# Scores of all chunks on VectorE, first loads and first Gram matrices spread over queues and banks, and a new order, in a fused deltanet and mixture-of-depths kernel

## The chip, the cores and the metric

The kernel runs on one core of a Trainium2 chip, in fp32. The metric is device time in microseconds, the median of the runs. The engines are PE (TensorE, matrix multiply), DVE (VectorE), ACT (ScalarE), POOL (GpSimd) and SP (SyncE, which issues DMAs).

## What is computed

Two blocks in a row. The first is a delta rule over 768 steps for 4 batches and 8 heads of width 48; its output, with the heads side by side, is x of width 384. The second takes, in each batch, the 128 tokens with the highest score, and runs these alone through a feed-forward network.

```python
k_n = k / (np.linalg.norm(k, axis=-1, keepdims=True) + 1e-06)
for t in range(S):
    kt, vt, bt = (k_n[:, :, t], v[:, :, t], beta[:, :, t, None])
    y[:, :, t] = np.einsum('bhd,bhde->bhe', q[:, :, t], state)
    v_old = np.einsum('bhde,bhd->bhe', state, kt)
    state = state + bt[:, :, :, None] * np.einsum('bhd,bhe->bhde', kt, vt - v_old)
x = np.ascontiguousarray(y.transpose(0, 2, 1, 3)).reshape(B, S, H * D)
scores = np.einsum('bsd,d->bs', x, w_gate)
for b in range(B):
    top_idx = np.argpartition(-scores[b], capacity)[:capacity]
    xe = x[b, top_idx]
    ye = np.maximum(xe @ w1, 0.0) @ w2
    g = 1.0 / (1.0 + np.exp(-scores[b, top_idx]))
    out[b, top_idx] = x[b, top_idx] + g[:, None] * ye
```

## The kernel before

**Tiling.** The sequence is cut into chunks of 64 steps. Two batches make a group, so there are 2 groups of 12 chunks: 24 chunks i, of 16 independent states (8 heads x 2 batches) each. Inside a chunk the 64 steps are solved at once, by inverting a triangular 64x64 matrix for each state. The inversions are done for four chunks together: six epochs e, of chunks 4e to 4e+3.

**Preparation of a chunk.** `load` (L655) brings k, q and v; PE transposes k (L666), ACT copies the result out as kt (L671). `products` (L716) multiplies the keys with each other, the Gram matrices, and with the queries. For epochs 1 to 5 the Gram matrices are copied to gs, spilled to DRAM and read back transposed as tile a. For epoch 0 this is done on the chip: `mm_g0` (L694) writes them to two PSUM banks, `out_g0` copies them to tile tt, one bank by DVE (L703, L708) and one by ACT (L703, L705, L706), and `turn_in` (L779) transposes them into a. The banks come from a ring "boot" of two entries, the banks prec and py, and the two halves of ap. A chunk gives its entry back when both engines have copied.

**An epoch.** The diagonal of a is read (L790 in epoch 0 on DVE, L825 on POOL afterwards), its root taken (ACT, L794), scales, strengths and a reciprocal formed (L830 to L839), a is scaled (L843), a table laid out (L808) and multiplied with it (L848, L849). This chain is POOL's, but for the root and the reciprocal. ACT lifts the result into PSUM (L856), and DVE eliminates: 30 pairs of a product (L878) and a subtraction (L885), each on the result of the one before. Then the solution is turned out (L866) and back (L898). POOL copies parts of it (lows, L1006, eight pieces, two for each chunk) for the join of the blocks of each chunk on PE (z, j) and ACT (L994, L1000).

**Recurrence of a chunk.** POOL scales v (L1032), PE multiplies with the state (L1040), DVE adds (L1047), PE applies the inverse (L1053), ACT copies (L1058), PE updates the state (L1064), and PE and ACT make x (L1080, L1091, L1097), which SP writes out (L1102). Then each token's score is the sum of x times w_gate: for chunks 0 to 21 POOL multiplies (L1114) and ACT sums (L1118), for the last two DVE does both in one instruction (L1110).

**Ranking and network, per group.** Each score is compared with all others of its batch by masks mk (POOL, L1199 with L1203; some by DVE), counted by ACT (L1217) and PE (sums, L1227), added up (L1233); the rank (L1265, L1266) is compared with a row of 1 to 128 (choose, L1269), which gives the indices (L1288, L1292, L1294). POOL gathers the chosen rows (L1309), DVE scores them again for the gate (rescore, L1297), PE runs both layers (mm_1 L1325, mm_2 L1339), DVE adds (L1344), POOL scatters (L1349).

**The order.** Nothing is scheduled by the compiler. Each operation is entered in a `Plan` with an engine, a cost, its dependencies and a due time, which two tables, SHIFT by kind of operation and PART by kind and place, move. A list scheduler lays the operations out on each engine with these numbers, and fills idle PE at the start with matmuls on a constant (filler, L577). The instruction streams are then written in that order, and each engine works through its own in order. DMA issues stand on SP's stream, some on ACT's or POOL's.

## Time and profile before

| | us |
| --- | --- |
| runs | 314.04, 312.94, 309.76 |
| median | 312.94 |
| the profiled execution | 311.51 |
| its span in the profile | 309.8 |
| PE, ACT, DVE, POOL busy in it | 266.2, 198.3, 187.3, 179.8 |
| mean granted clock of PE | 0.94 |

The span is what the profile shows, from the first to the last record; the time of an execution has some 1.7 us around it. A timeline row gives a start, a duration, engine, line, operation, what it writes and reads, and in brackets how long the engine was idle just before, with what released it. A group row gives the total, the mean of one in ns, and the idle time before the group's instructions. Line numbers are those of the kernel before.

### The profile page before, as it was taken

The numbers are of one execution on the slowest core, as the hardware profiler recorded it, in microseconds if no ns is written. First come the engines' busy times: TensorE is split into PE (matmuls) and PEld (weight loads), VectorE is DVE, ScalarE is ACT, GpSimd is POOL, SyncE is SP. The second block draws the span as 40 slices with busy tenths as digits, with TensorE's granted clock in tenths as the row PEclk, the third lists the DMA queues.
The fourth block names the chain that finished last, engine by engine and source line by source line (L and its number), as shares of the span: only waits on it lengthen the run. The fifth ranks groups of instructions, "written<-read, shape, count | busy, mean of one in ns | idle before, by whom it ended". The sixth has DMA issues, their size and how long they took to land.

```text
span 309.8 us, 14498 instructions
## 1 busy us (share of the span) xinstructions
PE 266.2 (86%) x6225; PEld 216.2 (70%) x6236; DVE 187.3 (60%) x518; ACT 198.3 (64%) x571; POOL 179.8 (58%) x258
## 2 busy tenths in 40 slices
...
GB/s 116 135 92 174 149 224 142 162 236 194 94 141 94 157 149 135 129 170 129 149 120 117 39 139 151 95 53 149 61 15 44 4 53 28 54 25 54 0 28 26
DMA packets 105889, 32.70 MB, mean 106 GB/s; under 512 B 98272, under 2 KB 102496, under 8 KB 105824
## 3 DMA queue, kind: packets, MB, share of 16 engines
...
q0 software_dynamic: 512, 1.57, 1.6%
q8 instruction: 49, 0.80, 1.1%
...
## 4 chain that ended last, share of the span: by engine, by line
PE 52%; ACT 15%; DVE 14%; issue 10%; POOL 4%; SPq 3%; DMA 2%; POOLq 0%; DVEq 0%; ACTq 0%
PE inv L716 6%; PE inv L666 6%; PE prec L1053 5%; DVE ap L885 5%; PE psta L1064 5%; DVE tmp L878 4%; PE ap L1339 4%; PE py L1080 4%; PE ap L1325 3%; PE py L1091 3%; ACT wbd L1058 3%; PE prec L1040 3%; PE inv L577 2%; SPq L655 2%; ACT tt L1000 2%
## 5 line engine op out<-in xcount | busy, mean ns | idle before, releaser
L885 DVE TENSOR_TENSOR ap<-ap,tmp 128x30 f32<-128x30 f32 (+9 forms) x180 | 60.8, 338 | 10.0 <-ACT a L861 3.8
L878 DVE TENSOR_TENSOR tmp<-a,ap 128x30 f32<-128x30 f32 (+9 forms) x180 | 58.8, 326 | 8.5 <-ACT ap L856 2.3
L738 POOL TENSOR_TENSOR p<-p,up 128x512 f32<-128x512 f32 x24 | 30.4, 1270 | 17.0 <-ACT p L732 16.9
L1199 POOL TENSOR_SCALAR mk<-rep 128x64 bf16<-128x64 f32 (+11 forms) x22 | 27.7, 1257 | 14.6 <-PE inv L1227 6.2
L1047 DVE TENSOR_TENSOR v<-v,prec 128x384 f32<-128x384 f32 x22 | 12.1, 549 | 32.6 <-ACT tt L1000 14.3
L1053 PE MATMUL prec<-v,tt 64*64 64x48 f32 x768 | 27.8, 220 | 4.2 <-POOL v L1032 1.5
L1053 PEld LDWEIGHTS prec<-v,tt 64*64 64x64 f32 x768 | 24.8, 134 | 8.5 <-DVE v L1047 3.7
L1058 ACT COPY wbd<-prec 64x384 f32<-64x384 f32 x48 | 22.7, 472 | 10.6 <-PE prec L1053 10.0
L1000 ACT COPY tt<-inv 32x128 f32<-32x128 f32 x96 | 24.4, 255 | 6.1 <-PE inv L993 4.5
L1006 POOL COPY tt<-tt 32x256 f32<-32x256 f32 x48 | 20.2, 422 | 11.9 <-DVE tt L866 8.4
L1032 POOL TENSOR_TENSOR v<-v,nnT 128x384 f32<-128x384 f32 x24 | 19.7, 831 | 11.6 <-DVE ap L885 9.7
L1064 PE MATMUL psta<-wbd,k 128*48 128x96 f32 x352 | 21.2, 264 | 4.9 <-ACT wbd L1058 4.7
L1114 POOL TENSOR_TENSOR prod<-x,wg 128x384 f32<-128x384 f32 x22 | 22.3, 1016 | 4.2 <-ACT x L1097 2.9
L1071 ACT COPY s<-psta 64x384 f32<-64x384 f32 x44 | 20.8, 472 | 4.2 <-PE psta L1064 3.6
L577 PE MATMUL inv<-warm 128*128 128x512 bf16 x57 | 20.3, 462 | 2.8 <-DVE warm L591 2.1
L1064 PEld LDWEIGHTS psta<-wbd,k 128*48 128x48 f32 x352 | 16.1, 130 | 8.5 <-ACT wbd L1058 7.6
L1349 POOL DMA_INDIRECT out_dram<-oe,idx x4 | 4.1, 1018 | 30.5 <-DVE oe L1344 24.9
L716 PE MATMUL inv<-qt,kt 48*64 48x64 f32 x768 | 19.1, 232 | 2.8 <-ACT qt L671 1.7
L1091 PE MATMUL py<-wbd,p 128*64 128x96 f32 x384 | 21.5, 255 | 0.0
L666 PE MATMUL inv<-ident,k 128*128 128x128 f32 x96 | 17.7, 315 | 3.5 <-issue 2.4
L1080 PE MATMUL py<-s,qt 128*64 128x96 f32 x352 | 19.7, 254 | 1.1 <-issue 1.0
L716 PEld LDWEIGHTS inv<-qt,kt 48*64 48x64 f32 x768 | 15.3, 141 | 6.4 <-ACT qt L671 3.0
(160 smaller groups left out, 633.0 us busy)
## 6 DMA issues: line engine op xcount, KB each, us to landing
...
q<-in_q_dram SPq DMA_DIRECT2D x48, 96.0 KB, 3.6
v<-in_v_dram SPq DMA_DIRECT2D x48, 96.0 KB, 3.3
k<-in_k_dram SPq DMA_DIRECT2D x44, 96.0 KB, 3.6
...
```

Source lines behind the costliest of these rows:

```text
L666: nc.tensor.transpose(ps[:, r * P:(r + 1) * P], x[:, 2 * r:2 * r + 2].rearrange("p b d -> p (b d)"), ident)
L716: nc.tensor.matmul(bank(keys[rt])[half[par], r], lhsT=kt[ds[rt], r, half[par]], rhs=x[ds[rt], r, half[par]], start=True, stop=True)
L738: nc.gpsimd.tensor_tensor(out=t, in0=t, op=ALU.mult, in1=up[:, None, :].to_broadcast([P, GP, C]))
L878: nc.vector.tensor_tensor(out=view(), op=ALU.mult, in0=got("a", e)[:, j + 1:, j:j + 1].to_broadcast([P, w, j]), in1=blocks[:, j:j + 1, :j] ...
L885: nc.vector.tensor_tensor(out=a[:, j + 1:, :j], in0=a[:, j + 1:, :j], in1=view(), op=ALU.subtract)
L1000: nc.scalar.copy(to[lo[par], :, int(w == "jb"), HC:], view(w)[lo[par]])
L1053: nc.tensor.matmul(pw[half[par], a], lhsT=tt[half[par], ch * GP + a], rhs=x[half[par], a], start=True, stop=True)
L1058: nc.scalar.copy(wb[half[par], :, par], pw[half[par]])
L1064: nc.tensor.matmul(psta[ds[a % 2], a // 2], lhsT=t[:, a, :D], rhs=wb[:, a].rearrange("p h d -> p (h d)"), start=(c == 0 and a < 2), stop=True,
L1080: nc.tensor.matmul(pyv[half[bb], h4, :, par], lhsT=qt[:, bb * 2 + h4, half[par]], rhs=s_old[:, bb * 2 + h4, par], start=(h4 == 0 and par = ...
L1091: nc.tensor.matmul(pyv[half[bb], h4, rt], lhsT=t[:, a], rhs=wb[:, a], start=(c == 0 and h4 == 0 and rt == 0), stop=True, skip_group_check= ...
L1199: nc.gpsimd.tensor_scalar(out=mk[:, :(j + 1) * C].rearrange("p (j c) -> p j c", c=C), in0=rep[:, :j + 1, :C], scalar1=rep[:, j, C:], scala ...
```

## The change

Line numbers from L790 on are 8 higher in the changed kernel, those of L738 and L716 5 higher. It does five things.

- The loads of k for chunks 0 and 1 go wholly to SP's queue, those of chunks 2 and 3 to ACT's; before, each of the four was split in halves between the two.
- The first Gram matrices of even chunks use the banks prec and py, those of odd chunks the first half of ap for DVE's copy and a bank of the ring inv for ACT's.
- The copies of the off-diagonal blocks by ACT become an operation of their own, `out_side` (L714), due 12 us later; the join's z of epoch 0 depends on it.
- All 24 scores are the single instruction on DVE (L1118).
- The planner has other costs, landing times and starts for each engine, other due times for the first operations, and new tables SHIFT and PART.

```diff
-LAND = 2.6
+LAND, EARLY, LATER = 2.4, 1.6, 6.0
+BEGIN = {"SP": 0.8, "ACT": 2.1, "DVE": 6.9, "POOL": 7.5, "PE": 2.1}
...
 SHIFT = {
-    "ACT:counts": -8.3, "ACT:ej": -53, "ACT:ez": -35.5, "ACT:gate0": 7.5, "ACT:lift": -50.6,
+    "ACT:counts": -2.9, "ACT:ej": -14.2, "ACT:ez": -3.1, "ACT:gate0": 8.6, "ACT:lift": -6.3,
...
-            self.lands.append(self.moved + LAND)
+            self.lands.append(self.moved + (LAND if t > LATER else EARLY))
...
-            free.setdefault(op.eng, 0.0)
+            free.setdefault(op.eng, BEGIN.get(op.eng, 0.0))
...
-    rings["boot"] = [[prec, py], [ap[:, m] for m in range(2)]]
-    plan.ring("boot", 2)
+    plan.ring("b0", 1)
+    rings["ap0"] = [ap[:, 0]]
+    plan.ring("ap0", 1)
...
+        def boot(rt):
+            x = [prec, py][rt] if i % 2 == 0 else got("inv", i, "boot") if rt else got("ap0", i)
+            return x[:, :GI * C].rearrange("p (r t) -> p r t", t=C)
+
...
                     if rt:
-                        put(to[hi[par], :, HC:], ps[hi[par], :, HC:])
-                        put(to[lo[par], :, :HC], ps[lo[par], :, HC:])
+                        put(to_g[hi[par], :, rt, HC:], ps[hi[par], :, HC:])
...
+        def out_side():
+            for par in range(2):
+                nc.scalar.copy(to_g[lo[par], :, 1, :HC], boot(1)[lo[par], :, HC:])
...
-        n["lk"] = sp(0.7 if first else 1.36,
-                     load(i, "k", (nc.sync, nc.scalar) if first else (nc.sync,) * 2),
-                     prio=u - 30, take=[("k", i)], dmas=2, room=None if first else 1.0)
-        if first:
-            act(0.7, lambda: None, [], u - 30)
+        if i in (2, 3):
+            n["lk"] = act(1.36, load(i, "k", (nc.scalar,) * 2), prio=u - 90, take=[("k", i)],
+                          dmas=2)
+        else:
+            n["lk"] = sp(1.36, load(i, "k", (nc.sync,) * 2), prio=u - (60 if first else 30),
+                         take=[("k", i)], dmas=2, room=None if first else 1.0)
...
-            n["g"] = pe(0.75, mm_g0, [n["ek"]], u, take=[kb], hard=True, ins=16 * GI)
-            n["eg"] = [dve(1.15, out_g0(0), [n["g"]], u, give=[kb], hard=True),
-                       act(1.0, out_g0(1), [n["g"]], u, give=[kb], hard=True)]
+            kb = [[("b0", i)], [("ap0", i), ("inv", i, "boot")]][i % 2]
+            n["g"] = pe(0.62, mm_g0, [n["ek"]], u - 100, take=kb, hard=True, ins=16 * GI)
+            n["eg"] = [dve(1.4, out_g0(0), [n["g"]], u - 100, give=kb[:1], hard=True),
+                       act(1.05, out_g0(1), [n["g"]], u - 100, give=kb[-1:], hard=True)]
+            n["sg"] = act(0.52, out_side, [n["g"]], u + 12, give=kb[-1:])
...
-            last = pool(2.5, scale_p, [s["sc"]], u)
-            last = pool(2.7, columns, [last, s["mb"]], u)
+            last = pool(1.95, scale_p, [s["sc"]], u)
+            last = pool(3.1, columns, [last, s["mb"]], u)
...
-        n["z"] = pe(0.36, z, [*s["to"], s["tb"]], u, take=[key["z"], ("zt", i)],
+        n["z"] = pe(0.36, z, [*s["to"], s["tb"], n.get("sg") if first else None], u, take=[key["z"], ("zt", i)],
...
-        late = i >= NU - 2
+        late = True
```

The body that `late` selects was there before, for the last two chunks:

```python
def score():
    if late:
        nc.vector.scalar_tensor_tensor(
            out=junk, in0=got("x", i // 2)[:, i % 2], scalar=1.0, in1=wg,
            op0=ALU.mult, op1=ALU.mult, accum_out=scr[g][:, c:c + 1])
        return
    nc.gpsimd.tensor_tensor(out=got("prod", i), in0=got("x", i // 2)[:, i % 2], in1=wg,
                            op=ALU.mult)
```

**ACT, the head.** Copies out of the first transposes (kt) and the first Gram matrices (into tt1_126), before; ap_143 is the bank pair ap, py_142 the bank py, and the waits are on counters of the engines named. The row of chunk 1's Gram matrices waits for DVE.

```order
L671 COPY kt2_86<-inv2_140 128x512 [waits PE_49]
L703 COPY tt1_126<-ap_143 32x4x32 [waits DVE_49,PE_49]
L705 COPY tt1_126<-ap_143 32x4x32
L706 COPY tt1_126<-ap_143 32x4x32
L703 COPY tt1_126<-ap_143 32x4x32
L705 COPY tt1_126<-ap_143 32x4x32
L706 COPY tt1_126<-ap_143 32x4x32
L671 COPY kt3_87<-inv1_139 128x512 [waits PE_49]
```

The same place after: inv1_139 is a bank of the ring inv.

```order
L670 COPY kt2_86<-inv2_140 128x512 [waits PE_49]
L670 COPY kt1_85<-inv0_138 128x512
L714 COPY tt1_126<-py_142 32x4x32 x2
L705 COPY tt1_126<-inv1_139 32x4x32 [waits PE_49]
L707 COPY tt1_126<-inv1_139 32x4x32
L705 COPY tt1_126<-inv1_139 32x4x32
L707 COPY tt1_126<-inv1_139 32x4x32
L705 COPY tt1_126<-py_142 32x4x32 [waits PE_49]
L707 COPY tt1_126<-py_142 32x4x32
L705 COPY tt1_126<-py_142 32x4x32
L707 COPY tt1_126<-py_142 32x4x32
L670 COPY kt3_87<-inv2_140 128x512
```

Chunk 1's copies now come out of a bank of inv and wait for PE alone; a chunk has four copies in this place where it had six, and the two off-diagonal ones (L714) stand apart and later.

**POOL, from the end of epoch 4 to the start of epoch 5's elimination.** Before: tt0_125 is epoch 4's solution, a1_114 and mb1_122 are epoch 5's tiles, p2_103 and p0_101 products that are masked (L738), both_134 the gathered rows.

```order
L1032 TENSOR_TENSOR v3_81<-v3_81,nnT1_168 128x384
L1114 TENSOR_TENSOR prod0_131<-x0_127,wg_163 128x384
L1006 COPY tt0_125<-tt0_125 32x8x32 x8
L738 TENSOR_TENSOR p2_103<-p2_103,up_155 128x512
L738 TENSOR_TENSOR p0_101<-p0_101,up_155 128x512
L1309 DMA both_134<-out_0_dram,idx0_185 128x384
L825 TENSOR_SCALAR nrm_166<-a1_114 128x32
L830 TENSOR_SCALAR nrm_166<-nrm_166 128x32
L832 TENSOR_TENSOR bh1_171<-nrm_166 128x32
L839 TENSOR_TENSOR bh1_171<-bh1_171,bt_145 128x32
L843 TENSOR_TENSOR a1_114<-a1_114,bh1_171 128x1024
L808 AFFINE_SELECT mb1_122<-bh1_171 128x1024
```

After:

```order
L1317 DMA both_134<-out_0_dram,idx0_185 128x384
L833 TENSOR_SCALAR nrm_166<-a1_114 128x32
L1317 DMA both_134<-out_0_dram,idx1_186 128x384
L838 TENSOR_SCALAR nrm_166<-nrm_166 128x32
L840 TENSOR_TENSOR bh1_171<-nrm_166 128x32
L847 TENSOR_TENSOR bh1_171<-bh1_171,bt_145 128x32
L851 TENSOR_TENSOR a1_114<-a1_114,bh1_171 128x1024
L816 AFFINE_SELECT mb1_122<-bh1_171 128x1024
L856 TENSOR_TENSOR mb1_122<-mb1_122,a1_114 128x1024
L857 TENSOR_SCALAR mb1_122<-bh1_171 128x32
L1014 COPY tt0_125<-tt0_125 32x8x32 x2
L1040 TENSOR_TENSOR v3_81<-v3_81,nnT1_168 128x384
```

The lows (L1006, now L1014) stood ahead of two masks, the first gather and the chain from the diagonal (L825, now L833) to the columns (L849, now L857); now both gathers and the whole chain stand ahead of them, and the product of a score (L1114) is gone.

**DVE, the end of epoch 4's elimination.** Before: a0_113 is epoch 4's tile, the last pair is followed by the turning out and back (L866, L898), the last sum of the ranking of group 0 (L1233), the rank (L1265, L1266) and the choice (L1269).

```order
L878 TENSOR_TENSOR tmp_172<-a0_113,ap_143 128x30
L885 TENSOR_TENSOR ap_143<-ap_143,tmp_172 128x30
L866 STREAM_TRANSPOSE tt0_125<-a0_113 128x16x32
L898 STREAM_TRANSPOSE mb0_121<-a0_113 128x32x32
L1233 TENSOR_TENSOR csum0_161<-csum0_161,inv2_140 128x12
L1265 TENSOR_TENSOR rank_180<-count0_178 128x12
L1266 TENSOR_TENSOR rank_180<-rank_180,csum0_161 128x12
L1269 TENSOR_TENSOR sel0_133<-iota_r_151,rank_180 128x1536
L1047 TENSOR_TENSOR v1_79<-v1_79,prec_141 128x384
```

After, the choice (L1277), a score (L1118), the indices of both batches (L1300, L1302) and an addition (L1055) stand between the elimination's steps, with seven pairs of the elimination still to end behind them:

```order
L1055 TENSOR_TENSOR v2_80<-v2_80,prec_141 128x384
L886 TENSOR_TENSOR tmp_172<-a0_113,ap_143 128x198
L1277 TENSOR_TENSOR sel0_133<-iota_r_151,rank_180 128x1536
L893 TENSOR_TENSOR ap_143<-ap_143,tmp_172 128x9x22
L1118 SCALAR_TENSOR_TENSOR junk_177,scr1_160<-x0_127,wg_163 128x384
L886 TENSOR_TENSOR tmp_172<-a0_113,ap_143 128x184
L1300 TENSOR_REDUCE idxf0_181<-inv2_140 128x1
L1302 CAST idx0_185<-idxf0_181 128x1
L893 TENSOR_TENSOR ap_143<-ap_143,tmp_172 128x8x23
L1300 TENSOR_REDUCE idxf1_182<-inv1_139 128x1
L1302 CAST idx1_186<-idxf1_182 128x1
L886 TENSOR_TENSOR tmp_172<-a0_113,ap_143 128x168
```

The choice has moved from behind the turning back to among the last pairs; further on both rescores stand ahead of the turning out.

## Rows read from the trace of the kernel before

**Rows 1.** The page: busy time by engine, and the chain's shares.

```profile
PE 266.2 (86%) x6225; PEld 216.2 (70%) x6236; DVE 187.3 (60%) x518; ACT 198.3 (64%) x571; POOL 179.8 (58%) x258
...
PE 52%; ACT 15%; DVE 14%; issue 10%; POOL 4%; SPq 3%; DMA 2%; POOLq 0%; DVEq 0%; ACTq 0%
```

**Rows 2.** Stretches: span; PE, PEld, DVE, ACT, POOL busy; clock, DMA share, GB/s.

```profile
184.00:206.00 22.00, 17.59 (x584) 15.08 (x583) 9.22 (x21) 16.53 (x48) 18.99 (x24) 0.92 0.46 91
```

**Rows 3.** Timeline of DVE around both gaps: start, duration, what, idle before.

```profile
111.14 2.06 DVE L898 STREAM_TRANSPOSE mb<-a 128x1024 f32<-128x1024 f32 x1
...
131.27 0.20 DVE L878 TENSOR_TENSOR tmp<-a,ap 128x30 f32<-128x30 f32 x1 [0.56 <-ACT ap L856]
...
186.10 2.03 DVE L898 STREAM_TRANSPOSE mb<-a 128x1024 f32<-128x1024 f32 x1
187.99 0.15 DVE L1233 TENSOR_TENSOR csum<-csum,inv 128x12 f32<-128x12 f32 x1
...
188.54 1.99 DVE L1269 TENSOR_TENSOR sel<-iota_r,rank 128x1536 bf16<-128x1536 f32 x1
...
205.96 0.20 DVE L878 TENSOR_TENSOR tmp<-a,ap 128x30 f32<-128x30 f32 x1 [1.77 <-ACT ap L856]
```

**Rows 4.** Timeline of POOL around both gaps.

```profile
113.12 3.49 POOL L1006 COPY tt<-tt 32x256 f32<-32x256 f32 x8
...
119.01 0.32 POOL L825 TENSOR_SCALAR nrm<-a 128x32 f32<-128x32 f32 x1
...
181.13 2.20 POOL L1199 TENSOR_SCALAR mk<-rep 128x768 bf16<-128x768 f32 x1 [2.74 <-ACT mute L1217]
...
186.31 4.90 POOL L1006 COPY tt<-tt 32x256 f32<-32x256 f32 x8 [0.85 <-DVE tt L866]
...
195.43 0.31 POOL L825 TENSOR_SCALAR nrm<-a 128x32 f32<-128x32 f32 x1
```

**Rows 5.** DMA issues of k: KB each, us to landing; and the queues' first.

```profile
k<-in_k_dram SPq DMA_DIRECT2D x44, 96.0 KB, 3.6
...
k<-in_k_dram ACTq DMA_DIRECT2D x4, 96.0 KB, 4.6
...
0.80 2.96 SPq L655 DMA_DIRECT2D k<-in_k_dram  x4
...
2.06 0.74 ACTq L655 DMA_DIRECT2D k<-in_k_dram  x1
```

**Rows 6.** Timeline of PE and DVE in the head.

```profile
2.08 4.65 PE L577 MATMUL inv<-warm 128*128 128x512 bf16 x11 [2.08 <-DVE warm L591]
...
18.09 1.92 DVE L779 STREAM_TRANSPOSE a<-tt 128x1024 f32<-128x1024 f32 x1 [1.11 <-ACT tt L705]
...
22.07 0.18 DVE L798 TENSOR_SCALAR nrm<-nrm 128x32 f32<-128x32 f32 x1 [1.59 <-ACT nrm L794]
```

**Rows 7.** Groups: ACT's copies of odd chunks: total, mean ns, idle before.

```profile
L703 ACT COPY tt<-ap 32x128 f32<-32x128 f32 x4 | 1.0, 256 | 2.0 <-DVE tt L708 1.1 <-PE prec L694 0.9
```

**Rows 8.** Groups: scores, rescores and additions.

```profile
L1114 POOL TENSOR_TENSOR prod<-x,wg 128x384 f32<-128x384 f32 x22 | 22.3, 1016 | 4.2 <-ACT x L1097 2.9 <-ACT junk L1118 1.0
L1118 ACT ACTIVATE junk<-prod 128x384 bf16<-128x384 f32 x22 | 11.6, 529 | 0.2
L1110 DVE SCALAR_TENSOR_TENSOR junk<-x,wg 128x384 bf16<-128x384 f32 x2 | 1.1, 554 | 4.1 <-ACT x L1097 4.1
L1297 DVE SCALAR_TENSOR_TENSOR junk<-both,wg 128x384 bf16<-128x384 f32 x4 | 3.1, 769 | 2.4 <-DMA both<-out_dram,idx 2.3
L1047 DVE TENSOR_TENSOR v<-v,prec 128x384 f32<-128x384 f32 x22 | 12.1, 549 | 32.6 <-ACT tt L1000 14.3 <-ACT kt L671 8.3 <-PE prec L1040 6.2
```

**Rows 9.** Timeline of POOL and DVE where a rescore took longest.

```profile
199.29 1.27 POOL L808 TENSOR_SCALAR_AFFINE_SELECT mb<-bh 128x1024 f32<-128x1024 f32 x1
...
199.63 1.33 DVE L1297 SCALAR_TENSOR_TENSOR junk<-both,wg 128x384 bf16<-128x384 f32 x1 [2.32 <-DMA both<-out_dram,idx]
```

**Rows 10.** Timeline of PE in the tail, the first layer.

```profile
282.89 5.62 PE L1325 MATMUL inv<-xeT,w_sb 128*128 128x128 f32 x48 [0.35 <-ACT xeT L1319]
```

More of the change, by code (lines that the diff above doesn't have):

```diff
@@ L20 @@
 LANES = 8
-LAND = 2.6
+LAND, EARLY, LATER = 2.4, 1.6, 6.0
+BEGIN = {"SP": 0.8, "ACT": 2.1, "DVE": 6.9, "POOL": 7.5, "PE": 2.1}
 SHIFT = {
-    "ACT:counts": -8.3, "ACT:ej": -53, "ACT:ez": -35.5, "ACT:gate0": 7.5, "ACT:lift": -50.6,
-    "ACT:lift_p": 0.8, "ACT:out_beta": 16.1, "ACT:out_g": -18.8, "ACT:out_g0": 3.8,
-    "ACT:out_h": 31.6, "ACT:out_p": 3, "ACT:out_rep": -47.8, "ACT:out_s": -0.7, "ACT:out_x":
-    2.5, "ACT:root": -13.4, "ACT:spot": 25.3, "ACT:total": 9.8, "DVE:<lambda>": 6.6,
-    "DVE:above": -4.1, "DVE:choose": -18.4, "DVE:diag": -11.8, "DVE:final": 10.3,
-    "DVE:gate1": 0.6, "DVE:invert": -10.4, "DVE:mul": -5.6, "DVE:order": 12.3, "DVE:out_g0":
-    -4.3, "DVE:out_idx": -22, "DVE:out_o": 13.7, "DVE:scale": -41.7, "DVE:scales": -45.6,
-    "DVE:score": -0.5, "DVE:sub": 20.7, "DVE:turn_back": -32.8, "DVE:turn_in": -16.3,
-    "DVE:turn_n": 24.1, "DVE:turn_out": -35.8, "DVE:turn_out_p": -43.4, "DVE:unit": 8.7,
-    "PE:<lambda>": -60, "PE:jj": -7.6, "PE:mm_1": 9, "PE:mm_2": 11.9, "PE:mm_g0": 39,
-    "PE:mm_idx": -21, "PE:mm_q": 10.6, "PE:mm_r": 3.2, "PE:mm_s": -10.1, "PE:mm_w": 14,
-    "PE:spread": 3, "PE:sums": -7.4, "PE:turn_beta": 2.4, "PE:turn_x": -15.8, "PE:z": -3.1,
-    "POOL:above": -41.1, "POOL:columns": -30.1, "POOL:diag_p": 4.3, "POOL:gather": 9.7,
-    "POOL:lows": -26.5, "POOL:mask": 12.9, "POOL:scales_p": 1.5, "POOL:scatter": -2.4,
-    "POOL:score": 1.4, "POOL:strength": 0.1, "POOL:vh": -5.9, "SP:<lambda>": 12.2,
-    "SP:load_beta": -15.1, "SP:load_weights": -26.4, "SP:put": -0.5, "SP:spill": -8,
-    "SP:turn_in": 0.6, "load_k": 9.5, "load_q": 20.1, "load_v": 36.2, "out_k": -0.7,
-    "out_q": 3.9, "products_kt": 0.1, "turn_q": 1.9,
@@ new lines @@
+    "DVE:mul": -24.9, "DVE:order": -2.9, "DVE:out_g0": -51.9, "DVE:out_idx": -1.4,
+    "DVE:out_o": 8.7, "DVE:rescore": 47.4, "DVE:scale": 1, "DVE:scales": 38.8, "DVE:score":
+    -2.1, "DVE:sub": 17.3, "DVE:turn_back": -3.2, "DVE:turn_in": 8.2, "DVE:turn_out": 29.4,
+    "DVE:turn_out_p": 5.8, "DVE:unit": -22.8, "PE:<lambda>": -3.3, "PE:jj": -47, "PE:mm_1":
+    11.1, "PE:mm_2": 21.4, "PE:mm_g0": 0.7, "PE:mm_idx": -7.2, "PE:mm_p": 11.9, "PE:mm_q":
+    49, "PE:mm_r": 23.8, "PE:mm_s": 9.6, "PE:mm_w": 34.2, "PE:spread": 1.3, "PE:sums": 19.8,
@@ new lines @@
+    "PE:turn_beta": 49.4, "PE:z": 37.8, "POOL:above": -26.2, "POOL:columns": -8,
+    "POOL:diag_p": -12, "POOL:gather": -15.2, "POOL:lows": 20.1, "POOL:mask": 4.4,
+    "POOL:scale_p": 2.1, "POOL:scales_p": 6.6, "POOL:strength": 17.3, "POOL:table": 12.3,
+    "POOL:vh": -0.1, "POOL:zeros": 27.6, "SP:<lambda>": -9.9, "SP:load_weights": -39.5,
+    "SP:put": -10.3, "SP:spill": -1, "SP:turn_in": 10.5, "load_k": 18.9, "load_q": 52.1,
+    "load_v": 42.7, "out_k": 27.6, "out_q": -8.8, "products_kt": -50.1, "products_qt": 8.6,
@@ L42 @@
+    "turn_k": 7.5, "turn_q": 4.4,
 }
 PART = {
[L44 to L51 removed]
```

354 lines of the change are left out of this document (175 added, 179 removed), and 35 rows, old and new, of the table PART.

## The prediction

> **What bounds the kernel now.** I read the busy times of the page and its chain first, then a table of stretches, then the timelines of VectorE (DVE), GpSimd (POOL) and ScalarE (ACT) around the places that the change touches, and last the groups of instructions that it moves. PE is busy 266.2 of 309.8 us, no other engine over 198.3, and the chain that ended last is 52% PE, 15% ACT, 14% DVE [rows 1]. So 43.6 us in which PE does nothing are the most that new order alone can win, and no gain beside PE's work counts until it reaches PE. From 238 us on nothing but PE matters; the end is reached by shortening what PE waits for earlier. What it waits for is an elimination of 60 dependent DVE steps for each of six epochs, because the four chunks of an epoch can't start before it. Between two eliminations DVE is nearly free: in the stretch 184 to 206 it works 9.22 of 22 us and POOL 18.99 [rows 2]. There the reader is to see two wide gaps. After epoch 2 the transposition back starts at 111.14 and the first step of epoch 3 at 131.27: 20.13 us. After epoch 4 it is 186.10 to 205.96: 19.86 us [rows 3]. In both the next elimination waits for a chain on POOL, from the diagonal (L825) to the columns (L849), which starts late: behind the lows (L1006), masks and, after epoch 4, a gather (119.01; 195.43) [rows 4].
>
> **The change part by part.**
>
> *The head.* SP issues its loads of k from 0.80 us on, four in 2.96, and they land 3.6 us after their issue; ACT issues its first at 2.06 and they take 4.6 [rows 5]. Chunk 0, until now half on each, was whole at 2.06 + 4.6 = 6.7; whole on SP, its second part is issued near 1.5 and lands near 5.1. The fillers ahead of it, 11 that end at 6.73, 0.42 us each, become 6, which end near 4.6 [rows 6]. With the queue now two parts deep on SP I take -1.4 of the 1.6. ACT's copies of the first Grams wait 2.0 us behind DVE's copies that hold a bank of the shared ring [rows 7]; separate banks take that wait away: -2.0. Eight of 24 such copies of 0.256 us are put off, but six of these still stand ahead of the last main one: two fewer, -0.5. The new banks come from rings that the transposes of k use as well, a new wait that no row shows: between 0 and 2.0 (the old one's size); I take 0.8. So the transposition of the Grams, at 18.09, starts 3.1 us sooner; the root's wait of 1.59 at 22.07 [rows 6] partly goes, since fewer copies stand ahead of it: -0.9. Head: **-4.0**, bounds -1.9 (the new wait at 2.0, nothing at the root) and -4.8 (no new wait).
>
> *The scores.* POOL's 22 products (22.3 us) and ACT's 22 sums (11.6) go, and 22 scores on DVE come [rows 8]. What they free lies beside PE's work and wins nothing by itself. Each costs DVE at least 0.554 with two free engines (the two that it has already, L1110); the same form over gathered rows took 0.769 in the mean of four (L1297) [rows 8], and one of those 1.33, 199.63 to 200.96, while POOL's table ran from 199.29 to 200.56 [rows 9]. Upper bound, then, 0.554 and 1.33 together, 1.9 for a score wholly held. Most of these scores fall where POOL is busy, so I take the mean and its read of the sum: 0.80. The trace thus leaves open whether a DVE operation with two SBUF operands is slowed or fully held while POOL works. The Trainium skill, "GPSIMD Engine Reference", section "Key points", states that GpSimd shares its SBUF interfaces with VectorE and that they contend when a DVE instruction has two SBUF inputs, as the score has and the elimination's steps (one operand in PSUM) have not; that speaks against this part of the change, and the row of 1.33 agrees with it. It gives no duration, and if it held each score wholly the sum would be the third rival's.
>
> Inside the eliminations, where each operation of DVE pushes all later steps: epoch 1 has two scores (**+1.6**), epoch 2 four (**+3.2**), epoch 3 three and one addition L1047 of 0.549 (**+2.95**), the gap behind it one score more and one addition fewer (**+0.25**). Additions stood 32.6 us on DVE waiting, 14.3 of it for ACT [rows 8]; a score ahead of one fills some of that: **-1.0** by my judgement, bounds 0 and -3.
>
> *The gap after epoch 2.* In the new order the masks mk of 192 and 256 stand ahead of the lows sooner, so the lows start when the tile is turned, about 111.2, not 113.12 (-1.9), and two products of 1.0 (one ahead of the diagonal, one in the chain) are gone (-2.0): **-3.9**. The two scores in that gap lie beside POOL's chain.
>
> *The ranking of group 0 and the gap after epoch 4.* This is the largest term. Before, the choice (L1269, 1.99 us at 188.54), indices, and both rescores stood behind the turned-back tile. Now they stand inside epoch 4's last steps, which pushes its end: choice 1.9, three scores 2.4, two rescores 1.6, one addition 0.55, ranks, indices, reciprocal and the short transposition 1.5 by their rows together: **+8.0**. In exchange POOL's chain for epoch 5 is now ahead of the lows (4.90 us at 186.31 [rows 4]) and begins when the gathers are issued, near 9 us before the end of that stretch. It took 10.5 us from the diagonal at 195.43 to the first step at 205.96 [rows 3, 4]; with the second gather in it some 11.6, so it ends about when DVE is through with turning back (2.03), one addition (0.55), gates and one score (0.8). I take 4.7 us for the gap in place of 19.86: **-15.2**. The lows of epoch 4 then come later, by the chain they gave way to: chunks 16 to 19 need them, and if they weren't covered they would cost at most the chain's 10 us; PE has epoch 4's first products, mm_1 and sums there, so I take nothing, and keep the rest for the range.
>
> *Epoch 5 and the end.* Three scores (+2.4), one rescore and one sum fewer (-0.9): **+1.5**. From its end to chunk 20 nothing changes. Nine matmuls of the first FFN half are no longer before chunk 20 but after it; a row of 48 records took 5.62 us, 0.117 each [rows 10], two records make one matmul: +2.1; the sums of group 1 no longer stand behind one that waits, -1.0: **+1.1**.
>
> *Planner costs, landings, due times* only set the order; their effect is in the terms above.
>
> **Sum**: -4.0 + 1.6 + 3.2 + 2.95 + 0.25 - 1.0 - 3.9 + 8.0 - 15.2 + 1.5 + 1.1 = -5.5. The profiled execution took 311.5 us (its span 309.8 and 1.7 around it), and lies 1.4 below the runs' median of 312.94. 311.5 - 5.5 = **306.0 us**, 2.2% under the median. A measurement of this kernel tells about 2% from no change, 6.3 us: faster means below 306.7.
>
> **The rivals.**
>
> *The ranking isn't ready (same).* The new order asks for the choice of group 0 some 7 us ahead of where it asked before, but the last mask (L1199) came only at 181.13, 2.74 us behind ACT's counts [rows 4], and its last sum is added at 187.99 [rows 3]. DVE would then stand inside epoch 4, with all later steps behind it. Against it: the products off POOL and the sums off ACT make the masks' round quicker, and 187.99 is late partly because the turning stood ahead. Masks not a bit earlier would mean a wait of about 4 to 6 us, of which I count 5: 306.0 + 5 = **311**. Equally the head's win could be lost in the second epoch's own waits; the time is then about the same.
>
> *The order works better than its parts (faster).* Scores at the low bound, 0.55 in place of 0.80, on the 15 that stand in eliminations: -3.7; waits filled by scores -3 in place of -1.0: -2.0; the head at its bound -0.8: -6.5 in all, **299.5**. For it speaks that ACT and POOL lose 34 us of work in a kernel in which both are near two thirds busy.
>
> *POOL holds the scores (slower).* One mechanism: each score stands until POOL's current instruction is over, at 1.9 us in place of 0.80. The 15 scores of the eliminations then cost 15 x 1.1 = 16.5 us more: 306.0 + 16.5 = **322.5**. For it the 1.33 of [rows 9]; against it the mean of four at 0.769, and that POOL with fewer products has more free moments. It decides from about 0.8 us more than I take, 1.6 a score: 306.0 + 15 x 0.87 = 319, the bound of slower.
>
> That the copies still wait (banks not separate in fact) is a part of the first rival: +2.0, 308.
>
> **How the numbers follow.** Forecast, by its own range 303 to 309: 0.42, of which 0.25 under 306.7. First rival 0.27, second 0.21, third 0.10. Faster: 0.25 + 0.21 = 0.46; same: 0.17 + 0.27 = 0.44; slower 0.10. The range for 8 in 10 is 298 to 314: it holds the forecast, the first rival and most of the second, and leaves out the third and the outer end of the second.
>
> **What would show it.** Right: turning of the first Grams near 15 us; no wait of ACT's Gram copies on DVE; scores of 0.7 to 0.9 us; the gap after epoch 4's turning back near 5 us and epoch 4's stretch near 32 long in place of 24.6; the gap after epoch 2 near 16; the tail from the last chunk's product unchanged within 1 us. Wrong: an idle stretch of DVE ahead of the choice (first rival); scores of 0.55 (second) or above 1.6 (third); a chunk 16 or 17 that waits for the lows, which I price at nothing.

## The result, and the profile after

The changed kernel takes 317.83 us in the median of 20 runs (312.80 to 323.42), the kernel before 312.39 in its 20. Ratios here and below compare the fast runs alone: in some of its executions every kernel is in a slower state, and the medians and ranges in us hold both. The ratio is 1.0137, with an interval of 1.0093 to 1.0181: slower by 1.4%, where 306.0 was forecast. The profiled execution took 317.08 us, its span 315.1.

First the page, as in [rows 1].

```profile
PE 271.5 (86%) x6226; PEld 221.1 (70%) x6241; DVE 204.9 (65%) x562; ACT 187.3 (59%) x527; POOL 161.0 (51%) x236
...
PE 47%; DVE 21%; ACT 9%; issue 8%; POOL 6%; DMA 4%; SPq 3%; POOLq 0%; DVEq 0%; ACTq 0%
```

POOL and ACT have lost 18.8 and 11.0 us of work, DVE has gained 17.6, and DVE's share of the chain has gone from 14 to 21%. The 22 new scores would be 12.2 us at the 0.554 of [rows 8]; the rest of the growth has to be looked for. The groups that answer to [rows 8]:

```profile
L1118 DVE SCALAR_TENSOR_TENSOR junk<-x,wg 128x384 bf16<-128x384 f32 x24 | 21.5, 894 | 4.4 <-ACT x L1105 4.4
L1305 DVE SCALAR_TENSOR_TENSOR junk<-both,wg 128x384 bf16<-128x384 f32 x4 | 4.7, 1176 | 0.0
L1055 DVE TENSOR_TENSOR v<-v,prec 128x384 f32<-128x384 f32 x22 | 12.1, 550 | 32.2 <-ACT ap L864 10.3 <-ACT zt L992 9.3 <-PE prec L1048 8.2
L705 ACT COPY tt<-inv 32x128 f32<-32x128 f32 x4 | 1.0, 256 | 0.2 <-PE ap L696 0.2
```

A score takes 0.894 us in the mean, a rescore 1.176, an addition what it took. The last row answers to [rows 7]: ACT's copies of odd chunks no longer wait for DVE.

Where the time went is read from the first step of each elimination (product on 128x30). DVE's timeline after, with the turnings back (L906):

```profile
25.31 0.20 DVE L886 TENSOR_TENSOR tmp<-a,ap 128x30 f32<-128x30 f32 x1
...
52.78 0.21 DVE L886 TENSOR_TENSOR tmp<-a,ap 128x30 f32<-128x30 f32 x1 [0.15 <-issue]
...
82.52 0.17 DVE L886 TENSOR_TENSOR tmp<-a,ap 128x30 f32<-128x30 f32 x1
...
115.40 2.03 DVE L906 STREAM_TRANSPOSE mb<-a 128x1024 f32<-128x1024 f32 x1
...
134.87 0.20 DVE L886 TENSOR_TENSOR tmp<-a,ap 128x30 f32<-128x30 f32 x1 [1.15 <-issue]
...
171.45 0.20 DVE L886 TENSOR_TENSOR tmp<-a,ap 128x30 f32<-128x30 f32 x1 [2.77 <-ACT ap L864]
...
206.95 2.00 DVE L906 STREAM_TRANSPOSE mb<-a 128x1024 f32<-128x1024 f32 x1
...
210.03 0.19 DVE L886 TENSOR_TENSOR tmp<-a,ap 128x30 f32<-128x30 f32 x1
```

The first steps of the kernel before that [rows 3] leave out:

```profile
26.95 0.20 DVE L878 TENSOR_TENSOR tmp<-a,ap 128x30 f32<-128x30 f32 x1
...
53.99 0.18 DVE L878 TENSOR_TENSOR tmp<-a,ap 128x30 f32<-128x30 f32 x1
...
82.42 0.18 DVE L878 TENSOR_TENSOR tmp<-a,ap 128x30 f32<-128x30 f32 x1
...
159.79 0.20 DVE L878 TENSOR_TENSOR tmp<-a,ap 128x30 f32<-128x30 f32 x1 [0.55 <-issue]
```

| stretch, from first step to first step | before | after | moved | forecast |
| --- | --- | --- | --- | --- |
| start to epoch 0 | 26.95 | 25.31 | -1.6 | -4.0 |
| epoch 0 to 1 | 27.04 | 27.47 | +0.4 | 0 |
| epoch 1 to 2 | 28.43 | 29.74 | +1.3 | +1.6 |
| epoch 2 to 3 | 48.85 | 52.35 | +3.5 | -0.7 |
| epoch 3 to 4 | 28.52 | 36.58 | +8.1 | +3.2 |
| epoch 4 to 5 | 46.17 | 38.58 | -7.6 | -7.2 |
| epoch 5 to the end of the span | 103.84 | 105.07 | +1.2 | +2.6 |

The forecast's -1.0 for filled waits belongs to no one row. The largest term came out: epoch 4's own stretch and the gap behind it. What failed are the head and the stretches of epochs 2 and 3.

### The profile page after: what moved, and what is told of

The parts are those of the page before. It is cut to its first block, busy times and chain, and to the rows that moved or that the text cites. A ratio compares the mean times of both kernels' runs of the same rounds, so it can differ in the third digit from the quotient of the medians.

```text
span 315.1 us, 14493 instructions
## 1 busy us (share of the span) xinstructions
PE 271.5 (86%) x6226; PEld 221.1 (70%) x6241; DVE 204.9 (65%) x562; ACT 187.3 (59%) x527; POOL 161.0 (51%) x236
## 4 chain that ended last, share of the span: by engine, by line
PE 47%; DVE 21%; ACT 9%; issue 8%; POOL 6%; DMA 4%; SPq 3%; POOLq 0%; DVEq 0%; ACTq 0%
DVE ap L893 6%; DVE tmp L886 6%; PE inv L721 5%; PE inv L665 5%; PE ap L1333 4%; PE prec L1061 4%; PE psta L1072 4%; PE ap L1347 4%; PE py L1099 3%; PE prec L1048 3%; DVE junk L1118 3%; PE py L1088 2%; DVE v L1055 2%; POOL mk L1207 2%; PE inv L1333 2%
## 5 line engine op out<-in xcount | busy, mean ns | idle before, releaser
L1207 POOL TENSOR_SCALAR mk<-rep 128x64 bf16<-128x64 f32 (+11 forms) x22 | 27.8, 1263 | 33.5 <-ACT rep L1199 21.6
L743 POOL TENSOR_TENSOR p<-p,up 128x512 f32<-128x512 f32 x24 | 32.0, 1338 | 24.3 <-ACT p L737 23.0
L1055 DVE TENSOR_TENSOR v<-v,prec 128x384 f32<-128x384 f32 x22 | 12.1, 550 | 32.2 <-ACT ap L864 10.3
L1040 POOL TENSOR_TENSOR v<-v,nnT 128x384 f32<-128x384 f32 x24 | 19.8, 829 | 15.8 <-DMA v<-in_v_dram 14.1
L1014 POOL COPY tt<-tt 32x256 f32<-32x256 f32 x48 | 19.7, 410 | 12.9 <-ACT qt L670 5.4
L576 PE MATMUL inv<-warm 128*128 128x512 bf16 x58 | 22.1, 466 | 3.9 <-DVE warm L590 2.1
L1118 DVE SCALAR_TENSOR_TENSOR junk<-x,wg 128x384 bf16<-128x384 f32 x24 | 21.5, 894 | 4.4 <-ACT x L1105 4.4
L1072 PE MATMUL psta<-wbd,k 128*48 128x96 f32 x352 | 20.4, 261 | 3.7 <-ACT wbd L1066 3.6
L1048 PE MATMUL prec<-s,kt 128*64 128x96 f32 x352 | 20.4, 261 | 2.5 <-ACT s L1079 2.2
L665 PE MATMUL inv<-ident,q 128*128 128x128 f32 x96 | 17.3, 308 | 5.6 <-DMA q<-in_q_dram 5.2
L670 ACT COPY qt<-inv 128x512 f32<-128x512 f32 x24 | 14.1, 585 | 11.3 <-PE inv L665 10.1
```

The lines of the kernel that those rows point to most:

```text
L665: nc.tensor.transpose(ps[:, r * P:(r + 1) * P], x[:, 2 * r:2 * r + 2].rearrange("p b d -> p (b d)"), ident)
L743: nc.gpsimd.tensor_tensor(out=t, in0=t, op=ALU.mult, in1=up[:, None, :].to_broadcast([P, GP, C]))
L1048: nc.tensor.matmul(pr[half[par], a * 2 * D:(a + 1) * 2 * D], lhsT=kt[:, a, half[par]], rhs=s_old[:, a, par].rearrange("p r d -> p (r d)"), ...
L1072: nc.tensor.matmul(psta[ds[a % 2], a // 2], lhsT=t[:, a, :D], rhs=wb[:, a].rearrange("p h d -> p (h d)"), start=(c == 0 and a < 2), stop=True,
L1118: nc.vector.scalar_tensor_tensor(out=junk, in0=got("x", i // 2)[:, i % 2], scalar=1.0, in1=wg, op0=ALU.mult, op1=ALU.mult, accum_out=scr[g ...
L1207: nc.gpsimd.tensor_scalar(out=mk[:, :(j + 1) * C].rearrange("p (j c) -> p j c", c=C), in0=rep[:, :j + 1, :C], scalar1=rep[:, j, C:], scala ...
```

## The experiments

Four theories were set against each other. **H**: DVE can't run an instruction with two operands in SBUF while POOL runs one of its own, so the scores are held, and that is the loss. **O**: the loss is the two late starts, of epochs 3 and 4. **Q**: the eliminations share DVE's queue with additions and scores that wait for PE, so an earlier start only waits later. **C**: TensorE's clock, which drops where PE ran dry. R and S belong to single runs. All kernels but two are the changed kernel with one edit; where an edit moves instructions, the rest of the order is untouched. "Before" on the same chips was 310.3 to 311.8 us.

**The hold, seen in the trace.** DVE and POOL of the changed kernel, three scores with what POOL ran:

```profile
110.55 2.49 POOL L743 TENSOR_TENSOR p<-p,up 128x512 f32<-128x512 f32 x2 [1.05 <-ACT p L737]
...
112.06 1.40 DVE L1118 SCALAR_TENSOR_TENSOR junk<-x,wg 128x384 bf16<-128x384 f32 x1
...
142.25 1.24 POOL L1207 TENSOR_SCALAR mk<-rep 128x384 bf16<-128x384 f32 x1
...
142.69 0.55 DVE L1118 SCALAR_TENSOR_TENSOR junk<-x,wg 128x384 bf16<-128x384 f32 x1
...
165.66 2.35 POOL L856 TENSOR_TENSOR mb<-mb,a 128x1024 f32<-128x1024 f32 x1
...
166.10 2.34 DVE L1118 SCALAR_TENSOR_TENSOR junk<-x,wg 128x384 bf16<-128x384 f32 x1
```

The first ends at 113.46, POOL's product at 113.04; the third ends at 168.44, POOL's columns at 168.01. Each ends 0.42 us behind POOL's instruction, whenever it began. The second lies wholly beside a comparison with one operand and takes 0.55. All 24 scores fit this: 0.55 to 0.67 alone or beside comparisons and copies, 0.76 to 0.99 where a held one began late, 1.27 to 2.34 where it began early. The kernel before shows it too: its two held rescores end 0.40 and 0.41 us behind POOL's instruction, the first of them in [rows 9] (200.96 behind 200.56).

**Scores out of PSUM.** The score reads x where PE left it, so one operand is in PSUM. (An entry of MOVES names an operation by kind and number, and then the operation that it is put directly behind; the list is written shorter here.)

```diff
-                    out=junk, in0=got("x", i // 2)[:, i % 2], scalar=1.0, in1=wg,
+                    out=junk, in0=py[:, :DM], scalar=1.0, in1=wg,
...
+MOVES = [("DVE:score", i, "ACT:out_x", i) for i in range(24)]
```

> The changed kernel, but each score reads x where PE has left it, in the PSUM bank py, in place of ACT's copy in SBUF, and stands right behind that copy in the order, so it has one SBUF operand. Theory H (DVE with two SBUF operands and POOL exclude each other): all 24 scores take 0.5 to 0.7 us, also those beside POOL's masks of p and its columns, where the changed kernel's took 0.9 to 2.3; the rescores, which still read SBUF, keep 1.2 to 2.4. If the scores' hold is most of the loss the time falls by 4 us or more, to 314 or less. [...]

Measured: 315.48 us (313.84 to 317.24), 1.0129 of before, interval 1.0065 to 1.0192. Its scores, and one beside a POOL instruction with two operands:

```profile
L1118 DVE SCALAR_TENSOR_TENSOR junk<-py,wg 128x384 bf16<-128x384 f32 x24 | 13.3, 555 | 31.6 <-ACT x L1105 31.4
...
68.25 1.91 POOL L851 TENSOR_TENSOR a<-a,bh 128x1024 f32<-128x1024 f32 x1
...
69.19 0.56 DVE L1118 SCALAR_TENSOR_TENSOR junk<-py,wg 128x384 bf16<-128x384 f32 x1 [0.21 <-ACT x L1105]
```

The hold is gone from every score (21.5 to 13.3 us), and the rescores, still out of SBUF, keep it (1.58 and 1.28 beside POOL's chain). But DVE now stood 31.4 us behind ACT's copy, since the edit also put the scores earlier, and H's 314 or less was missed. So the place was put back:

```diff
-MOVES = [("DVE:score", i, "ACT:out_x", i) for i in range(24)]
+MOVES = []
...
+        if ops.index(x) > ops.index(y):
+            ops.remove(x)
+            ops.insert(ops.index(y), x)
```

Here x is a score and y the next chunk's first write of the bank: only a score that stood behind that write moves.

> As the kernel whose scores read PSUM, but each score stays at the place that the changed kernel gives it (only no later than the next chunk's first write of the bank), not right behind ACT's copy, where DVE stood 31 us behind that copy. Theory H: scores of 0.56 and no such wait: 4 to 7 us below the changed kernel, 311 to 314. Theory Q (what bounds epochs 3 and 4 is that their steps stand in one queue with additions and scores that wait for PE's recurrence): 315 to 318, the shorter scores turn into longer waits ahead of additions.

Measured: 311.34 us (10 runs, 307.86 to 314.40), 0.9941 of before, interval 0.989 to 0.9991: H's range, 6.5 us below the changed kernel and at or just below the kernel before. A part of the 6.5 goes with the clock, whose median was 0.93 in these runs and 0.922 in the changed kernel's; at about the same clock it is 3.7 to 5.0 us (313.43 at 0.929 and 311.96 at 0.924, against 317.08 at 0.928 and 316.99 at 0.924). In the profiles the eliminations of epochs 1, 2 and 4, from the first step to the turning back, are 1.6, 1.8 and 3.8 us shorter. Its group of scores, with a third of the wait:

```profile
L1118 DVE SCALAR_TENSOR_TENSOR junk<-py,wg 128x384 bf16<-128x384 f32 x24 | 13.2, 551 | 9.9 <-ACT x L1105 7.1 <-PE py L988 2.7
```

**The scores left out.**

```diff
-                nc.vector.scalar_tensor_tensor(
-                    out=junk, in0=got("x", i // 2)[:, i % 2], scalar=1.0, in1=wg,
-                    op0=ALU.mult, op1=ALU.mult, accum_out=scr[g][:, c:c + 1])
+                nc.vector.tensor_copy(
+                    scr[g][:, c:c + 1],
+                    got("x", i // 2)[:, i % 2, :1])
```

> The changed kernel with each score left out and a copy of the first column of x (0.1 us) in its place, so other tokens are chosen; all else as it is. This prices the scores as a whole: 24 x 0.89 us on DVE, some 14 us of them between elimination steps. H: 8 to 14 us less, 304 to 310. Q: most of it comes back as waits, 313 to 317.

Measured: 306.94, 308.56, 313.95 and 314.56 us, too few and too spread for a ratio. The first two lie in H's range, the others in Q's. All four are within or just outside the range of the kernel with its scores out of PSUM (307.86 to 314.40). So most of what the scores cost the changed kernel is their hold; the two lowest runs have a mean of 307.75, that kernel's seven that its ratio uses 310.02, and whether an unheld score costs something too is not settled.

**The scores back on POOL and ACT.**

```diff
+            if i >= NU - 2:
...
+            nc.gpsimd.tensor_tensor(out=pr, in0=xx, in1=wg, op=ALU.mult)
+            nc.scalar.activation(junk, pr, AF.Copy, accum_out=acc)
```

> The changed kernel with its order as it is, but chunks 0 to 21 scored as before: a product on POOL and a sum on ACT, issued where the single DVE instruction stood. Theory H (the loss comes from scores that DVE can't finish while POOL runs an instruction with two operands; 24 took 0.89 us in the mean, up to 2.34): the eliminations of epochs 1, 2 and 3 shrink by 2 to 4 us each and the time falls to 311 to 314. Theory O (the loss comes from two places where the new order lets the next elimination start late, epochs 3 and 4): the eliminations shrink, but the products of 1.0 us lengthen POOL's chain by as much, and the time stays at 316 to 320.

Measured: 329.84 us (326.99 to 331.10), 1.0619 of before: both ranges missed. It is a poor control. In this order ACT's sum stands right behind POOL's product, and ACT waits for it:

```profile
L1123 ACT ACTIVATE junk<-prod 128x384 bf16<-128x384 f32 x22 | 11.5, 523 | 21.7 <-POOL prod L1122 21.5
```

What it does show: the order counts on POOL and ACT being free of the scores, and gets worse when they are not.

**The two late starts.** Epoch 3's lift put directly behind the columns, with six pairs of steps ahead of an addition and a score:

```diff
+MOVES = [("ACT:lift_p", 5, "POOL:columns", 2), ("ACT:lift_p", 4, "ACT:lift_p", 5),
+         ("DVE:mul", 90, "ACT:lift_p", 4), ("DVE:sub", 90, "DVE:mul", 90),
...
```

> Only epoch 3's start is put in another order: both halves of its lift stand on ACT right where POOL's columns end, ahead of the join's copies and a spill copy, and six pairs of steps stand on DVE ahead of an addition and a score. Theory O: epoch 3's first step comes 16 us after epoch 2's turning back has begun, in place of 19.5, and the time falls by 2 to 4 us, to 314 to 316. Theory H: what is won there is lost again in later scores, less than 1.5 us in all.

Measured: 323.80 us (321.01 to 326.61), 6 us above the changed kernel and outside both ranges. Epoch 3 did start at 129.4 in place of 134.87, 15.4 us behind the turning back as O wanted, but its steps then took 34.4 us, not 27.8 (in an execution with a mean clock of 0.882, where the changed kernel's had 0.928). Epoch 4's columns put ahead of two masks:

```diff
+MOVES = [("POOL:columns", 3, "POOL:scale_p", 3), ("ACT:lift_p", 6, "ACT:lower", 5),
+         ("ACT:lift_p", 7, "ACT:lift_p", 6),
+         ("DVE:mul", 120, "DVE:turn_back", 3), ("DVE:sub", 120, "DVE:mul", 120),
...
```

> Only epoch 4's start is put in another order: POOL's columns stand right behind the scaling, ahead of two masks of 1.7 and 1.9 us, the lift behind epoch 3's last copy, six pairs of steps ahead of a score and a sum. Theory O: epoch 4's first step comes 2 to 3 us after the turning back of epoch 3 has begun, in place of 7.2; the time falls by 3 to 5 us, to 313 to 315. A rival to it, R (the ranking of group 0 is what epoch 4 ends on): DVE then waits the same 3 to 5 us ahead of the choice, and the time stays at 317 to 319. Theory H: less than 1.5 us.

Measured: 318.13 us (314.75 to 321.20). Epoch 4 started at 160.7 in place of 171.45, and ended at 203.2 in place of 203.8: 42.4 us long, not 32.4. The waits of DVE inside it, PE's stretch meanwhile, and the same stretch of the changed kernel (columns as in [rows 2]):

```profile
177.29 0.56 DVE L1118 SCALAR_TENSOR_TENSOR junk<-x,wg 128x384 bf16<-128x384 f32 x1 [6.08 <-ACT x L1105]
182.26 0.56 DVE L1055 TENSOR_TENSOR v<-v,prec 128x384 f32<-128x384 f32 x1 [4.08 <-PE prec L1048]
...
164.00:182.00 18.00, 17.18 (x415) 14.17 (x415) 7.58 (x23) 12.27 (x40) 9.86 (x13) 0.53 0.27 76
```

```profile
164.00:182.00 18.00, 15.82 (x517) 11.97 (x519) 14.23 (x36) 14.43 (x43) 14.67 (x19) 0.91 0.43 104
```

The 10.2 us are two waits, for the output of chunk 12 and the state product of chunk 13, ahead of a score and an addition and not of the choice. So it is not R, though the time lies in R's range. It fits Q, but C is in it as well: PE is busy nearly throughout and gets through 415 records where the changed kernel's got through 517; it ran at the lower of its two clock levels (1.2 GHz) for 17 us of this stretch, and the changed kernel's for 3.4. Before the clock fell PE had stood 2.62 us waiting for a copy of ACT's (1.65 us for a load in the changed kernel). Both together:

> Both edits together. Theory O: they add, 5 to 9 us, to 309 to 313. R: the win of the first alone, 314 to 316. H: 316 or more.

Measured: 323.14 us (316.51 to 323.71), too spread for a ratio, and in none of its four runs near O's 309 to 313. And epoch 4's early start with the scores out of PSUM:

> Scores out of PSUM at their old places, and epoch 4's start early as in the kernel that put the columns ahead of two masks. H with O: both wins add, 306 to 311, at or below the kernel before. Q: 313 to 317, epoch 4's stretch over 38 us long again.

Measured: 314.95 us (10 runs), 1.0076 of before, interval 1.0025 to 1.0128; epoch 4's stretch was 40.1 us long. That is Q's range, and 3.6 us worse than without the early start. PE's stretch:

```profile
164.00:182.00 18.00, 17.28 (x482) 14.20 (x484) 7.87 (x24) 11.65 (x37) 8.82 (x13) 0.62 0.25 70
```

Here too PE was at the lower level for 13.7 us. O has fallen twice: an earlier start of epoch 4 doesn't reach the end. Whether Q alone takes it back, or the longer time at the lower clock, these runs don't separate.

**The clock.** 46 dummy matmuls ahead of four waits of PE:

```diff
+FILL = {("turn_", 14): 20, ("PE:mm_w", 3): 9, ("PE:jj", 10): 9, ("turn_", 37): 7,
+        ("PE:mm_r", 14): 10}
```

(The second place had no free bank and got none.)

> The changed kernel with 46 dummy matmuls of 0.2 us on PE, ahead of four of the waits in which it stood idle for 1.6 to 5.2 us (40 to 45, 124 to 127, 162 to 163, 203 to 205 us). C: the granted clock behind them stays at full, the mean rises from 0.928 to 0.95 or more, and the time falls by 3 to 6 us, to 312 to 315. If the clock is only a companion of the waits, the mean clock rises but the time stays at 317 to 319.

Measured: 319.61 us (5 runs, 319.00 to 326.32), 1.0245 of before. The stretch 44 to 52 us, in the changed kernel and in this one:

```profile
44.00:52.00 8.00, 5.78 (x69) 3.62 (x74) 7.55 (x15) 2.24 (x5) 7.33 (x7) 0.57 0.99 189
```

```profile
44.00:52.00 8.00, 5.04 (x113) 2.85 (x113) 7.55 (x16) 3.63 (x9) 6.67 (x7) 1.00 1.08 142
```

There the dummies kept the clock at full, and epoch 1 still started 27.1 us behind epoch 0, where the changed kernel took 27.5: little waits for PE then. Further on other waits took their place, and the clock fell at other times. Its three lowest runs, 319.00 to 319.61, had mean clocks of 0.933 to 0.944, above the changed kernel's median of 0.922, and were no faster for it. So filling the waits isn't the remedy; C as the cause of single stretches is neither shown nor excluded.

**Parts of the change alone.** The kernel before with its scores on DVE, in its order:

```diff
-            if late:
+            if True:
```

> The kernel before with its order, only the scores of chunks 0 to 21 as one DVE instruction at the place where POOL's product stood, and no sum on ACT. H: scores of 0.8 to 0.9 us in the mean; 17 of them between elimination steps; each lengthens them, and the time rises by 3 to 6 us, to 315 to 318. Theory S (the scores on DVE gain where the order lets POOL and ACT use the time): it falls by 2 to 6 us, to 306 to 310. C: no change beyond 2 us unless the mean clock moves by 0.01 or more, about 1.8 us for each 0.01 as the changed kernel's 20 runs show.

Measured: 319.65 us (318.46 to 321.01), 1.0252 of before. The scores took only 0.609 us in the mean, hardly held, and yet it is 8 us slower; none of the ranges held that. So it is not the hold. Their place on DVE, ahead of steps, is the cause that suggests itself; it is not shown. Additions there waited 12.9 us for PE, 6.2 in [rows 8], and 5.2 of the 8.4 us by which the span is longer lie behind epoch 5's first step. The new code with the old tables:

> The changed kernel's code and planner costs with the kernel before's two tables, so that everything is placed by the old due times. If the code (head, scores) is a gain that the new order spoils, 304 to 310; if the code itself costs time, 315 or more whatever the tables; if the tables are fitted to their own code and carry over badly, 320 or more.

Measured: 325.62 us, 1.0479 of before. The last two of the three expectations hold that, so it shows only that the new code wins nothing in the old order, not whether the code costs time or the tables carry over badly. The kernel before with the new split of the first loads:

```diff
-                     load(i, "k", (nc.sync, nc.scalar) if first else (nc.sync,) * 2),
+                     load(i, "k", (nc.scalar if i in (2, 3) else nc.sync,) * 2),
```

> The kernel before with its order; only the first loads differ: both halves of k of chunks 0 and 1 are issued by SP and those of chunks 2 and 3 by ACT, at the old places. If the head's gain reaches the end: epoch 0 starts 1 to 1.5 us sooner and the time falls by as much, to 310 to 311.5. If the head is covered by what epochs 1 and 2 wait for: epoch 0 sooner, the time the same within 0.7.

Measured: 310.97 us (12 runs), ratio 1.001, interval 0.9966 to 1.0054. Chunk 0 was transposed at 5.82 us, 0.75 sooner, but chunk 1 had to be waited for, and epoch 0 started at 27.2. PE's rows:

```profile
5.82 0.60 PE L666 MATMUL inv<-ident,k 128*128 128x128 f32 x4
...
7.92 0.30 PE L666 MATMUL inv<-ident,k 128*128 128x128 f32 x1 [1.29 <-DMA k<-in_k_dram]
```

The split alone wins nothing, not even at epoch 0; so whether a gain there reaches the end isn't answered by it.

**The rescores.** Scores out of PSUM, and the last pair and both turnings of epoch 4 ahead of the rescores; then also six pairs of epoch 5 ahead of a score.

```diff
+MOVES = [("DVE:mul", 149, "DVE:sub", 148), ("DVE:sub", 149, "DVE:mul", 149),
+         ("ACT:lower", 7, "DVE:sub", 149), ("DVE:turn_out_p", 7, "ACT:lower", 7),
+         ("DVE:turn_back", 4, "DVE:turn_out_p", 7)]
```

> Scores out of PSUM at their old places, and on DVE epoch 4's last pair, turning out and turning back ahead of both rescores, which were the other two-operand instructions held by POOL's chain (1.23 and 2.37 us in the changed kernel). H: epoch 4's turning out comes 2 to 3 us sooner and chunk 16 with it, the time 1 to 3 us below the kernel with PSUM scores alone, 308.5 to 310.5. Q: epoch 5 starts no sooner, since POOL's columns and a score that waits for PE stand ahead of its first step: 310.5 to 312.5.

> The same, and the first six pairs of epoch 5 ahead of the score that waits for PE's write of x. H with O: epoch 5 starts 1 to 1.5 us sooner again: 307.5 to 310. Q: the score's group then waits longer behind the pairs, no gain: 310.5 to 312.5.

Measured: 314.95 us (309.24 to 317.60) and 317.51 (309.29 to 320.85), too spread for a ratio, and no gain to be seen: five of the six runs of each lie above both ranges, the lowest (309.24 and 309.29) in H's. In the first the rescores were down to 0.88 and 0.56 us and the turning out came 1.2 us sooner, but epoch 5 started at 206.6, behind this row:

```profile
206.13 0.56 DVE L1118 SCALAR_TENSOR_TENSOR junk<-py,wg 128x384 bf16<-128x384 f32 x1 [2.40 <-PE py L988]
```

In the second it started at 202.2, and took 31.2 us. Again the time went into a wait for PE; PE's clock was at its lower level from about 202 to 216 and from 202 to 215, so this too is Q or C.

## Why the prediction was wrong

The mechanism failed, and not only a size: by the sum the span was to shrink by 5.5 us, and it grew by 5.3. Of these 10.8 us, 4.3 lie in the gap after epoch 3, 3.2 in the gap after epoch 2, 2.4 in the head and 1.0 in waits that scores were to fill (additions waited 32.2 us, 32.6 before); the rest nearly cancels. What the experiments could win back, though, is the price of a score.

**The step that failed with an effect on the time is the price of a score.** The text took "the mean and its read of the sum: 0.80". There is no one price here: a score takes 0.55 or it ends 0.42 us behind POOL's instruction. 24 of them took 21.5 us where 13.2 would do. The 15 inside the eliminations took 14.5 where 12.0 was set down, and the two rescores inside epoch 4 3.6 where 1.6 was. The mean of all, 0.894 and 0.02 more with the read of the sum, is not far from 0.80. But a fixed price per score hid that the longest holds (1.86, 2.10, 2.34) are beside the columns and the scaling, the very chain that the next elimination waits for. With the hold removed the time was 311.34 in place of 317.83, of which 3.7 to 5.0 us remain at like clocks. This is the third rival's mechanism, given a chance of 0.10; its price was too high, since not every instruction of POOL holds (comparisons and copies don't). The rule of the Trainium skill that was weighed against this step ("GPSIMD Engine Reference", "Key points") agrees with the held scores and with those out of PSUM; that POOL's comparisons and copies hold little or nothing (0.55 to 0.67 beside them) it does not say. The Trainium skill's "Trainium Architecture — The Big Picture", section "What this means for kernel authors", adds that the pair of ports is locked and its bandwidth not split; the fixed 0.42 us behind POOL's end fits a lock.

**The gap after epoch 2** was to shrink by 3.9 us. POOL's part did: the columns end 14.1 us behind the turning back where it was 18.0. Then a step came that the prediction had not priced, ACT's lift. Rows of ACT and PE:

```profile
131.72 0.60 ACT L864 COPY ap<-mb 128x512 f32<-128x512 f32 x1
133.63 0.65 ACT L728 COPY gs<-inv 128x256 f32<-128x256 f32 x2 [1.31 <-PE inv L721]
134.17 0.61 ACT L864 COPY ap<-mb 128x512 f32<-128x512 f32 x1
...
126.79 0.26 PE L999 MATMUL inv<-zt,mb 32*32 32x32 f32 x1 [2.27 <-issue]
...
118.00:124.00 6.00, 5.12 (x256) 4.40 (x245) 1.49 (x5) 4.77 (x18) 4.77 (x9) 1.00 0.78 160
...
127.00:134.00 7.00, 7.00 (x132) 5.83 (x124) 1.03 (x3) 3.76 (x13) 3.21 (x3) 0.55 0.31 56
```

The lift's second half stands behind a copy that waits for PE, and PE, which had stood 2.27 us inside a run of matmuls, was at 0.55 of its clock. The gap is 19.5 us in place of 20.1.

**The gap after epoch 3** was set down at +0.25; from the last pair to the first step it grew by 4.6. I had not read POOL's order there: two masks now stand between the scaling and the columns.

```profile
159.12 2.23 POOL L851 TENSOR_TENSOR a<-a,bh 128x1024 f32<-128x1024 f32 x1
161.34 1.73 POOL L1207 TENSOR_SCALAR mk<-rep 128x576 bf16<-128x576 f32 x1
...
163.43 1.88 POOL L1207 TENSOR_SCALAR mk<-rep 128x640 bf16<-128x640 f32 x1
```

These two terms were wrong. But the experiments took both late starts away and won nothing, so a sum that adds gaps is wrong in a deeper way: an elimination that starts sooner can wait, in the same queue, for the chunk before it, and can change where PE runs dry and its clock falls. The prediction said "no gain beside PE's work counts until it reaches PE" and then did not ask it of each term.

**The head** was overestimated: 1.6 us, not 4.0. Chunk 0 was ready at 5.11 us as worked out, and the wait on DVE went; the turning came at 17.04, not 15, since the copies of later chunks still waited for PE's products.

**Epoch 4 and the gap behind it** were right in sum: its stretch grew by 7.8 (forecast 8.0), the gap behind the turning back shrank to 3.1 us (4.7), and between the last pair and the turning back 1.4 us were lost. In part that is luck: the scores and rescores inside the stretch took 7.6 us where 4.0 was set down, and what balanced it is not in the sum. The lows, priced at nothing, were right too: they began at 207.15, released by the turning out, when POOL's chain had been over for 0.84 us. From the last chunk's inverse product to the end nothing changed.

**The rivals.** "The ranking isn't ready" named a wait ahead of the choice; there was none.

**What stays open.** With the hold gone the time is 311.3, not 306. That starting epoch 3 or 4 sooner by these edits wins nothing is shown; whether the queue or the clock takes it back, and which wait of PE sets the pace of chunks 12 to 16, is not. In the changed kernel's 20 runs the time falls by 1.5 us for each 0.01 of mean clock, and its median clock is 0.922 against 0.935 in 43 runs of the kernel before: worked out, some 2.0 of the 5.4 us go with the clock. Whether the clock made them or followed the waits no run separates.
